# A long convolution and a feed-forward block on one core: a new early part, k and v in pieces, spectra of x in three groups, and a new written order

## The chip, the cores and the metric

The kernel runs on one core of a Trainium2 chip. The engines that matter here are TensorE (called PE in the profile, with its weight loads apart as PEld), VectorE (DVE), ScalarE (ACT), GpSimd (POOL) and SyncE (SP), which here only issues DMAs. The metric is device time in microseconds. The kernel before took 229.11 us, the median of three runs (227.98 to 230.42). The profile is of one further execution, which took 230.95 us.

## The reference, cut to what matters

The input `q` is [1, 2048, 640]; `k` and `v` have the same shape. All tensors are bf16.

```
def _A_ref(q, k, v, shift_k, ssm_k, ssm_D):
    # k_shift: four-tap causal filter of k along the sequence, a set of taps for each channel
    kv = k_shift * v
    # y: causal convolution of kv with ssm_k along the 2048 positions (by FFTs of length 4096)
    y = y + kv * ssm_D
    return q * y
def _B_ref(x, w1, b1, w2):          # 640 -> 1728 -> 640
    h = einsum("bsd,df->bsf", x, w1) + b1
    act = h * tanh(softplus(h))     # Mish
    return einsum("bsf,fd->bsd", act, w2)
x = q
h = x + _A_ref(_layernorm(x), k, v, shift_k, ssm_k, ssm_D)
out = h + _B_ref(_layernorm(h), w1, b1, w2)
```

## The kernel before, in words

The convolution is done as a Fourier transform by matmuls. The 2048 positions are split as 128 times 16, and the 640 channels into five chunks of 128, called `dc` 0 to 4. The filter `ssm_k` (called h) and the product kv (called x) go through the same two steps.

* `k1pe`: the filter's chunk (`kn`) is transposed, 16 transposes into one pair of PSUM banks; `k1ev` copies the two halves out to `kk`. Before that, `drow` turns the row `ssm_D` into a column with five one-column matmuls and `dadd` adds it to position 0 of the filter, so that the term `kv * ssm_D` costs nothing later.
* `s1pe` (line L280): step one, 16 matmuls for eight pairs of channels; four of these (`gi` 0 to 3) for each chunk. `s1ev` evicts a pair of banks (128x1024 in f32) to the buffer `B`.
* `s2pe` (L363): step two, one matmul for each of 128 frequencies and each group of chunks, against the matrix `G`, which `gb` builds from the table `R`. Chunks 0, 1 are one group of 64 columns, chunks 2, 3, 4 another of 96. `s2ev` evicts (128x1024 or 128x768) into `K` for the filter and into `X` for kv.
* `ktpe`/`ktev` (L314) transpose k; `shpe` (L333) does the four-tap filter with 32-row matmuls; `kv` (L341) multiplies by v on DVE and writes `kvb`, the input of step one for x.
* `d_sw`: DMAs within the chip's memory that write for each block of 16 channels a copy of the filter's spectrum with real and imaginary halves swapped (`KPS`). `pr` (L412, DVE) multiplies both copies by the spectrum of x; there are ten blocks of two halves.
* `i1pe` (L423, L424) and `i2pe` (L485) are the inverse transform, with evictions `i1ev` and `yev` (all evictions are line L185, on ACT or DVE).

Then come the rows. For each of 16 tiles T of 128 positions, `ln1` takes the statistics of x (L464), `lnx` normalises on ACT, `wb` and `h` form q*y and the residual, `ln2` takes statistics again, `dr` normalises, and the result is transposed: by PE for tiles 0 and 1 (`trpe`, `trev`), by DMA (`d_tr`, L553) for the others. The feed-forward block works in six units of 1, 1, 2, 4, 4, 4 tiles: `m1pe` (L573) and the activation `mi` (L580, ACT), then `m2pe` (L597), the last addition `res` (L616) and the store `d_o`.

PSUM has eight banks, used as four pairs for all evictions of 1024 columns (pair 0 is banks 0 and 1), or singly. A block of matmuls may start only when the pair it writes has been evicted.

The order of all this is not chosen at run time: a long string, `ORDER`, lists some 760 operations with their engine, their PSUM bank or pair, and for most DMAs an eviction behind which they are paced (`d_sw0_0:sp:@s1ev_h_4_0`). Each engine executes its operations strictly in that order; SP issues DMAs strictly in that order too, so a DMA that waits for its pace or its data holds up every later one. A dependence graph adds the semaphore waits.

```
for name, eng, slots, behind in _order():
    o = ops.pop(name)
    for x, s in zip(o.allocs, slots):
        x["slot"] = x["ring"][s]
    r = o.emit(eng)
    if behind:
        tc.add_manual_dep(r.ins, copies[behind].ins.name, info, reason="pace")
```

Of the kernel before, what the change touches and what calls it, by code (L numbers as in the profile page):

```python
# [15 lines left out]
P = 128  # L16
S = 2048
# [12 lines left out]
NGRP = len(GRP_DC)  # L30
KPE = 5
# [17 lines left out]
    "K": (O_K, 81920), "X0": (O_X, 16384), "X1": (O_KVB, 24576),  # L49
}  # L50
for _i, (_a, _b) in enumerate(GRP_DG):
    BUFS[f"B{_i}"] = (O_B + 256 * _a, 256 * (_b - _a))
# [117 lines left out]
def plan(v):  # L170
# [24 lines left out]
    def e_consts(e):  # L195
        v.nc.scalar.dma_start(v.consts[:], v.dram["consts"])
        v.nc.scalar.dma_start(v.buf("Drow", [P, D])[0:1], v.A_D.rearrange("(o d) -> o d", o=1))
    g.op("consts", "act", e_consts, w=["consts", "Drow"], kind="consts")
# [24 lines left out]
    if KPE:  # L223
        for h in range(2):
            dma(f"d_k{h}", 2048 * KC, lambda e, h=h: v.nc.sync.dma_start(
                v.buf("kna", [P, NT, KC])[:, 8 * h:8 * h + 8, :], v.A_k[0].rearrange("(p a) d -> p a d", a=NT)[:, 8 * h:8 * h + 8, 0:KC]), w=[("kna", h)])
    for h in range(2):
        dma(f"d_v{h}", 1.31e6, lambda e, h=h: v.nc.sync.dma_start(
            v.buf("v", [P, NT, D])[:, 8 * h:8 * h + 8, :], v.A_v[0].rearrange("(p a) d -> p a d", a=NT)[:, 8 * h:8 * h + 8, :]), w=[("v", h)])
# [6 lines left out]
    def e_pewarm(e):  # L236
        pw = bank(wrt)
        for i in range(8):
            v.nc.tensor.matmul(pw[:, 0:512], v.buf("warm", [P, 512])[:, 0:128], v.buf("warm", [P, 512]), start=True, stop=True)
# [6 lines left out]
    g.op("drow", "pe", e_drow, r=["Drow", "consts"], allocs=[drt], kind="drow")  # L246
# [9 lines left out]
    def e_pewarm2(e):  # L256
        for i in range(2):
# [3 lines left out]
    keep = g.op("pewarm2", "pe", e_pewarm2, r=["warm"], allocs=[wrt2], kind="pewarm2", after=[o for o in g.ops if o.name == "drow"])  # L261
# [4 lines left out]
    for i, (c0, c1) in enumerate(((0, 1), (1, 2), (2, 5))):  # L266
# [4 lines left out]
    def s1(st, dc, src, skey, bname, g0):  # L271
        for gi in range(4):
# [8 lines left out]
            g.op(f"s1pe_{st}_{dc}_{gi}", "pe", pe, r=["consts", (skey, gi // 2)], allocs=[rt], kind="s1pe")  # L281
# [6 lines left out]
    def k1(dc, grp):  # L288
        rt = alloc(D2)
        kk = f"kk{dc % 4}"  # L290

        def pe(e):
            pk = bank(rt, BF16).rearrange("p (t d) -> p t d", t=NT)
            for t2 in list(range(1, NT)) + [0]:
                v.nc.tensor.transpose(pk[:, t2, :], v.buf("kn", [P, NDC, S])[:, dc, t2:S:NT], v.ident)  # L295
        g.op(f"k1pe{dc}", "pe", pe, r=[("kn", dc), "consts"], allocs=[rt], kind="k1pe", after=[keep])
        for h in range(2):
            g.op(f"k1ev{dc}_{h}", EV, lambda e, h=h: ev(
                e, v.buf(kk, [P, 64, NT, 2])[:, 32 * h:32 * h + 32], bank(rt, BF16).rearrange("p (t d m) -> p d t m", t=NT, m=2)[:, 32 * h:32 * h + 32]),
                w=[(kk, h)], uses=[rt], kind="evb", arg=1024)  # L300
        s1("h", dc, lambda: v.buf(kk, [P, 64, NT, 2]), kk, f"B{grp}", GRP_DG[grp][0])
# [6 lines left out]
    for h in range(2):  # L308
        for dc in range(KPE):
# [5 lines left out]
            g.op(f"ktpe{dc}_{h}", "pe", pe, r=[("kna", h), "consts"], allocs=[rt], kind="ktpe")  # L315
# [36 lines left out]
    def s2(st, grp, dst, keys):  # L352

        d0, d1 = GRP_DG[grp]
        nd = d1 - d0
        nf, pitch, cost = SHAPE[nd]
        for ci in range(P // nf):
# [3 lines left out]
            def pe(e, rt=rt, f0=f0):  # L361
                for fl in range(nf):
                    v.nc.tensor.matmul(bank(rt)[:, fl * pitch:fl * pitch + nd], v.buf("G", [P, P, P])[:, f0 + fl, :], v.buf(f"B{grp}", [P, P, nd])[:, f0 + fl, :],  # L363
                                       start=True, stop=True)
            o = g.op(f"s2pe_{st}_{grp}_{ci}", "pe", pe, r=gall(f0, nf) + [f"B{grp}"], allocs=[rt], kind="s2pe", arg=nf * cost)
# [5 lines left out]
    def blocks(grp):  # L371
# [443 lines left out]
```

## Time and profile before

| what | value |
|---|---|
| median of three runs | 229.11 us (227.98 to 230.42) |
| the profiled execution | 230.95 us, its span 229.2 us |
| PE busy | 215.5 us (94%) |
| DVE busy | 149.0 us (65%) |
| ACT busy | 139.4 us (61%) |
| first eviction on ACT starts | 10.16 us |
| first matmul of the feed-forward block starts | 104.41 us |
| last matmul block ends | 225.8 us |

"Span" is from the first to the last instruction; the execution's own time is 1.75 us longer. Times in the trace count from the span's start. "Busy" of PE counts matmuls from their start to their modelled end, and as they are pipelined, a busy PE is not a PE at its peak. A timeline row gives start, length, engine, line, operation, shape and count, and in brackets the idle time ahead of it and who ended it. The granted clock is 1.00 in nearly all slices of the page, but the rate of the matmuls themselves tells more, as the prediction shows.

### The profile page before, as it was taken

The page shows a single profiled execution, that of the slowest core. Times are in us where ns is not written, and L with a number is a line of the kernel's source. Part 1 is how long each engine was busy: PE and PEld are TensorE (multiplying, and loading weights), DVE is VectorE, ACT ScalarE, POOL GpSimd, SP SyncE. Part 2 cuts the span into 40 slices and gives each one's busy share as a digit, 9 for nine tenths or more (in the row PEclk, how much of TensorE's full clock was granted, in tenths as well). Part 3 has the DMA queues.
Part 4 walks back from the last instruction along what each step waited for, and adds up shares of the span by engine and source line. Part 5 has one row for each costly group of instructions (what it writes and reads, how often), then busy time and mean ns, then how long its engine had stood idle before and what let it go on. Part 6 is the DMA issues. An engine that isn't in the chain of part 4 may idle for free.

```text
span 229.2 us, 6927 instructions
## 1 busy us (share of the span) xinstructions
PE 215.5 (94%) x3016; PEld 162.4 (71%) x3021; DVE 149.0 (65%) x274; ACT 139.4 (61%) x200; POOL 28.1 (12%) x60
## 2 busy tenths in 40 slices
PE   6899998979888999999999999999999999999994
PEld 2798888868787899998978764447557444577773
DVE  0469999999999999999999999965001200004131
ACT  2159998847999999999939367781350466100000
POOL 2120000000010000221233443522000000000000
PEclk9999999999999999999999999999999999999999
DMA  6999604845665777788230423424000100002021
GB/s 204 402 370 374 247 3 97 182 100 139 157 152 138 209 202 219 227 228 257 83 86 4 104 39 87 87 59 60 30 0 29 57 3 0 0 0 85 33 80 35
DMA packets 19872, 27.87 MB, mean 122 GB/s; under 512 B 10881, under 2 KB 14978, under 8 KB 19330
## 3 DMA queue, kind: packets, MB, share of 16 engines
q1 hardware_dynamic: 19536, 27.32, 41.0%
q8 instruction: 23, 0.38, 0.7%
q10 hardware_dynamic: 146, 0.11, 0.5%
q0 software_dynamic: 160, 0.01, 0.2%
q14 instruction: 7, 0.06, 0.1%
HBM read 17.27 MB, written 2.62 MB: 87 GB/s over the span
## 4 chain that ended last, share of the span: by engine, by line
PE 65%; ACT 14%; DVE 12%; DMA 4%; issue 3%; ACTq 0%; DVEq 0%
PE banks L597 26%; PE banks L573 23%; ACT arena L185 14%; PE banks L280 4%; DVE arena L412 4%; PE banks L363 3%; DVE arena L185 3%; PE banks L295 2%; DMA arena<-arena 2%; PE banks L333 2%; DMA arena<-in_A_ssm_D_dram 2%; DVE st L464 2%; DVE arena L341 2%; PE banks L576 1%; PE banks L485 1%
## 5 line engine op out<-in xcount | busy, mean ns | idle before, releaser
L185 ACT CAST arena<-banks 128x1024 bf16<-128x1024 f32 (+3 forms) x93 | 79.9, 985 | 16.5 <-PE banks L280 11.7
L597 PE MATMUL banks<-arena 128*128 128x320 bf16 (+2 forms) x448 | 61.7, 299 | 0.0
L580 ACT ACTIVATE arena<-banks,b1s 128x512 bf16<-128x512 f32 (+2 forms) x84 | 41.5, 535 | 29.7 <-PE banks L573 29.1
L573 PE MATMUL banks<-arena 128*128 128x512 bf16 (+2 forms) x395 | 58.2, 305 | 0.6 <-DVE nmr L473 0.3
L597 PEld LDWEIGHTS <-arena 128*128 128x128 bf16 x448 | 43.2, 98 | 18.1
L573 PEld LDWEIGHTS <-arena 128*128 128x128 bf16 x400 | 33.1, 98 | 23.7 <-issue 0.6
L616 DVE TENSOR_TENSOR arena<-banks,arena 128x640 bf16<-128x640 f32 x15 | 12.2, 816 | 56.4 <-PE banks L597 52.6
L185 DVE CAST arena<-banks 128x1024 bf16<-128x1024 f32 (+1 forms) x27 | 30.4, 1158 | 2.0 <-PE banks L280 1.3
L280 PE MATMUL banks<-consts,arena 128*64 128x128 bf16 x640 | 23.3, 230 | 2.6 <-ACT arena L185 1.1
L363 PE MATMUL banks<-arena 128*128 128x64 bf16 (+1 forms) x512 | 22.5, 199 | 2.7 <-ACT arena L185 2.4
L280 PEld LDWEIGHTS <-arena 128*64 128x64 bf16 x640 | 20.3, 116 | 4.7 <-issue 2.7
L363 PEld LDWEIGHTS <-arena 128*128 128x128 bf16 x512 | 19.9, 98 | 4.7 <-issue 3.6
L412 DVE TENSOR_TENSOR arena<-arena 128x2048 bf16<-128x2048 bf16 x20 | 22.9, 1216 | 0.2 <-DMA arena<-arena 0.2
L535 ACT ACTIVATE arena<-arena,nmr,r1v 128x640 bf16<-128x640 bf16 x16 | 14.3, 930 | 8.7 <-DVE nmr L473 7.5
L423 PE MATMUL banks<-a,arena 128*128 128x128 bf16 x160 | 18.8, 219 | 0.7 <-ACT arena L185 0.6
L424 PE MATMUL banks<-a,arena 128*128 128x128 bf16 x160 | 18.7, 219 | 0.0
L424 PEld LDWEIGHTS <-arena 128*128 128x128 bf16 x160 | 15.6, 98 | 0.9 <-issue 0.8
L423 PEld LDWEIGHTS <-arena 128*128 128x128 bf16 x160 | 15.6, 98 | 0.6 <-DVE arena L412 0.3
L185 DVE COPY arena<-banks 128x1024 bf16<-128x1024 bf16 (+1 forms) x17 | 10.7, 658 | 5.3 <-PE banks L295 4.5
L464 DVE BATCH_NORM_STATS2 st<-arena 128x6 f32<-128x320 bf16 x32 | 13.8, 474 | 0.0
L341 DVE TENSOR_TENSOR arena<-banks,arena 128x512 bf16<-128x512 f32 x20 | 12.3, 681 | 0.7 <-PE banks L333 0.3
L523 DVE BATCH_NORM_STATS2 st<-arena 128x6 f32<-128x320 bf16 x28 | 12.3, 480 | 0.2
(60 smaller groups left out, 139.6 us busy)
## 6 DMA issues: line engine op xcount, KB each, us to landing
arena<-arena SPq DMA_DIRECT2D x20, 256.0 KB, 3.0
arena<-in_A_ssm_k_dram SPq DMA_DIRECT2D x5, 512.0 KB, 6.4
arena<-in_A_k_dram SPq DMA_DIRECT2D x2, 1280.0 KB, 13.1
arena<-in_A_v_dram SPq DMA_DIRECT2D x2, 1280.0 KB, 19.6
arena<-in_A_q_dram SPq DMA_DIRECT2D x8, 320.0 KB, 3.2
out_dram<-arena SPq DMA_DIRECT2D x15, 160.0 KB, 1.8
arena<-in_B_w_dram SPq DMA_DIRECT2D x5, 432.0 KB, 4.4
arena<-in_B_w_dram SPq DMA_DIRECT2D x3, 480.0 KB, 5.1
```

What stands on the lines that cost most here:

```text
L185: v.copy = v.nc.scalar.copy(o, i) if e == "act" else v.nc.vector.tensor_copy(o, i)
L280: v.nc.tensor.matmul(pz[64 * ri:64 * ri + 64, gl, :], lhs, v.fcfs[:, ri, :], start=True, stop=True)
L341: v.nc.vector.tensor_tensor(v.buf(f"kvb{dc}", [P, 64, NT, 2])[:, q * 16:(q + 1) * 16], bank(rts[h])[:, i * 512:(i + 1) * 512].rearrange("p ...
L363: v.nc.tensor.matmul(bank(rt)[:, fl * pitch:fl * pitch + nd], v.buf("G", [P, P, P])[:, f0 + fl, :], v.buf(f"B{grp}", [P, P, nd])[:, f0 + f ...
L412: v.nc.vector.tensor_tensor(kk, xx.unsqueeze(1).to_broadcast([P, 2, 16, 64]), kk, ALU.mult)
L423: v.nc.tensor.matmul(pz[:, gl, :], v.buf(f"KP{b}", [P, 16, P])[:, 8 * h + gl, :], v.a12[:, 0, :], start=True, stop=False)
L424: v.nc.tensor.matmul(pz[:, gl, :], v.buf(f"KPS{b}", [P, 16, P])[:, 8 * h + gl, :], v.a12[:, 1, :], start=False, stop=True)
L464: v.nc.vector.bn_stats(v.st1[:, T % 4, q, :], x(T)[:, q * 320:(q + 1) * 320])
L535: g.op(f"lnx{T}", "act", lambda e: v.nc.scalar.activation(lnx(), x(T), ACT.Identity, scale=v.r1v[:, T:T + 1], bias=v.nmr1[:, T:T + 1]), r= ...
L573: v.nc.tensor.matmul(ph[:, 0:w], w1[:, dc, fc * P:(fc + 1) * P], lt[:, dc, T0 * P:T0 * P + w], start=(dc == 0), stop=(dc == NDC - 1))
L580: g.op(f"mi{u}_{fc}", "act", lambda e, fc=fc, rt=rt, ww=ww: v.nc.scalar.activation(ub()[:, fc, 0:ww], bank(rt)[:, 0:ww], ACT.Mish, bias=v. ...
L597: v.nc.tensor.matmul(bank(rt)[:, q * 512:q * 512 + b - a], lhs, w2()[:, wc, a:b], start=(fc == 0), stop=(fc == NFC - 1))
```

## The change

1. **The first chunk of the filter.** It is transposed in two blocks of eight (`k1pe0_0`, `k1pe0_1`) into single banks, each evicted by itself. Each copy covers half of the 16 values of the inner position for all channels, so all four `s1pe_h_0` blocks now need both copies. `ssm_D` is no longer added to this chunk ahead of the transposes; `dk0` adds the row to the evicted copy, in one partition, 128 elements. The other four chunks keep `drow` and `dadd`, and `drow` stands behind the first transposes.
2. **The warm-up.** Matmuls on a zeroed buffer run at the start: 8 and then 2 before (the 2 behind `drow`), 7 and 3 now, all ten in one go ahead of the first transposes.
3. **The identity apart.** The table `consts` came in one DMA; now the identity (128 columns) comes first in a DMA of its own, then `ssm_D`, then the rest.
4. **k and v** come in four DMAs each of 640 KB instead of two of 1280 KB, and those of k, v and `R` are no longer issued at once but paced behind evictions.
5. **The spectra of x** are made in three groups of chunks (0, 1 / 2, 3 / 4) of 64, 64 and 32 columns instead of two of 64 and 96. The filter keeps two groups. So `s2pe_x` has 384 matmuls instead of 256, and 20 evictions of 1024 columns instead of 8 of 1024 and 16 of 768.
6. **A new order** of everything, with the engine of many evictions chosen afresh. Up to the feed-forward block, two copies of `k1ev` and four more evictions of `s1ev` go from DVE to ACT, three copies of `ktev` from ACT to DVE, `trev0` (the first tile's transpose) to ACT, and two `yev2` evictions and three of the four `ln1` that stood there go behind it or change their place. `shpe4` and all of chunk 4 of x come late; one inverse block, `i2pe2_3`, now stands among the first unit's `m1pe` blocks; `m1pe` of the 4-tile unit of tiles 4 to 7 now follows one `m2pe` instead of two.

```
+X_DC = [[0, 1], [2, 3], [4]]
+X_DG = [(32 * c[0], 32 * c[-1] + 32) for c in X_DC]
...
-        v.nc.scalar.dma_start(v.consts[:], v.dram["consts"])
         v.nc.scalar.dma_start(v.buf("Drow", [P, D])[0:1], v.A_D.rearrange("(o d) -> o d", o=1))
+        v.nc.scalar.dma_start(v.consts[:, 128:424], v.dram["consts"][:, 128:424])
+    g.op("ident", "act", lambda e: v.nc.scalar.dma_start(v.consts[:, 0:128], v.dram["consts"][:, 0:128]), w=["ident"], kind="ident")
...
-        for h in range(2):
-            dma(f"d_k{h}", 2048 * KC, lambda e, h=h: v.nc.sync.dma_start(
-                v.buf("kna", [P, NT, KC])[:, 8 * h:8 * h + 8, :], ...
+        for h in range(4):
+            dma(f"d_k{h}", 1024 * KC, lambda e, h=h: v.nc.sync.dma_start(
+                v.buf("kna", [P, NT, KC])[:, 4 * h:4 * h + 4, :], ...
...
-        for i in range(8):
+        for i in range(7):
             v.nc.tensor.matmul(pw[:, 0:512], v.buf("warm", [P, 512])[:, 0:128], v.buf("warm", [P, 512]), start=True, stop=True)
...
-        for i in range(2):
+        for i in range(3):
...
-    keep = g.op("pewarm2", "pe", e_pewarm2, ..., after=[o for o in g.ops if o.name == "drow"])
+    keep = g.op("pewarm2", "pe", e_pewarm2, ..., after=[o for o in g.ops if o.name == "pewarm"])
...
-    for i, (c0, c1) in enumerate(((0, 1), (1, 2), (2, 5))):
+    for i, (c0, c1) in enumerate(((1, 2), (2, 5))):
...
+        if dc == 0:
+            for h in range(2):
+                rt = alloc(D1)
+                def pe(e, rt=rt, h=h):
+                    pk = bank(rt, BF16).rearrange("p (t d) -> p t d", t=8)
+                    for t2 in range(8 * h, 8 * h + 8):
+                        v.nc.tensor.transpose(pk[:, t2 - 8 * h, :], v.buf("kn", [P, NDC, S])[:, dc, t2:S:NT], v.ident)
+                g.op(f"k1pe{dc}_{h}", "pe", pe, r=[("kn", dc), "ident"], allocs=[rt], kind="k1pe", arg=8, after=[keep])
+                g.op(f"k1ev{dc}_{h}", EV, lambda e, h=h, rt=rt: ev(
+                    e, v.buf(kk, [P, 64, NT, 2])[:, :, 8 * h:8 * h + 8], bank(rt, BF16).rearrange("p (t d m) -> p d t m", t=8, m=2)),
+                    w=[(kk, ("t", h))], uses=[rt], kind="evb", arg=1024)
+            g.op("dk0", "dve", lambda e: v.nc.vector.tensor_tensor(
+                v.buf(kk, [P, 64, NT, 2])[0:1, :, 0, :], v.buf(kk, [P, 64, NT, 2])[0:1, :, 0, :],
+                v.buf("Drow", [P, D])[0:1, 0:128].rearrange("p (d m) -> p d m", m=2), ALU.add), r=["Drow"], w=[(kk, ("t", 0))], kind="tiny")
...
-        d0, d1 = GRP_DG[grp]
+        d0, d1 = (GRP_DG if st == "h" else X_DG)[grp]
...
-    for grp in range(NGRP):
-        d0, d1 = GRP_DG[grp]
+    for grp in range(len(X_DC)):
+        d0, d1 = X_DG[grp]
```

The new order begins as follows, against the old one's first lines:

```
-    d_kn0:sp consts:act small:pool warmset:dve d_kn2:sp pewarm:pe:0 tab:act d_kn4:sp d_kn1:sp d_kn3:sp d_k0:sp d_R0:sp d_k1:sp d_R1:sp drow:pe:0
-    d_v1:sp pewarm2:pe:1 dadd0:dve k1pe0:pe:1 d_v0:sp k1ev0_0:dve k1ev0_1:dve s1pe_h_0_0:pe:3 d_a12:sp s1pe_h_0_1:pe:0 s1ev_h_0_0:act diag:dve
+    ident:act consts:act tab:act small:pool d_kn0:sp warmset:dve d_kn2:sp pewarm:pe:0 d_kn1:sp d_kn4:sp d_kn3:sp pewarm2:pe:0 k1pe0_0:pe:1
+    k1pe0_1:pe:2 k1ev0_0:dve drow:pe:3 k1ev0_1:dve dk0:dve s1pe_h_0_3:pe:1 s1pe_h_0_0:pe:0 s1ev_h_0_3:act dadd0:dve diag:dve s1pe_h_0_2:pe:2
+    d_R0:sp:@k1ev0_1 s1ev_h_0_0:act s1ev_h_0_2:dve k1pe1:pe:1 s1pe_h_0_1:pe:0 k1ev1_0:dve s1ev_h_0_1:act dadd1:dve k1ev1_1:dve s1pe_h_1_1:pe:2
```

## The prediction

> **What bounds it now.** I read the busy time by stretches first: up to the first eviction's stage, the middle of the convolution, its later half, the feed-forward block.
>
> ```profile
> 9.00:57.00 48.00, 43.61 (x1274) 40.19 (x1276) 42.87 (x61) 37.30 (x43) 2.52 (x4) 1.00 0.64 201
> 57.00:104.40 47.40, 44.53 (x836) 41.11 (x831) 46.25 (x64) 47.36 (x58) 3.79 (x7) 1.00 0.72 191
> 104.40:225.80 121.40, 120.80 (x885) 77.92 (x887) 58.45 (x147) 53.24 (x100) 19.66 (x42) 1.00 0.21 54
> ```
>
> The columns are PE, PEld, DVE, ACT, POOL, granted clock, DMA share, GB/s. From 104.4 on PE has no gap: that part can't get shorter, and begins when it may. From 57 to 104.4 ACT is busy 47.36 of 47.40 us, DVE 46.25, PE 44.53: three full engines, ACT the fullest. Before 57 ACT loses time, so I went to its timeline.
>
> ```profile
> 10.16 1.01 ACT L185 CAST arena<-banks 128x1024 bf16<-128x1024 f32 x1 [6.89 <-PE banks L280]
> 11.87 1.93 ACT L185 CAST arena<-banks 128x1024 bf16<-128x1024 f32 x2 [0.69 <-PE banks L280]
> 15.72 1.01 ACT L185 CAST arena<-banks 128x1024 bf16<-128x1024 f32 x1 [1.93 <-PE banks L280]
> 17.44 7.61 ACT L185 CAST arena<-banks 128x1024 bf16<-128x1024 f32 x8 [0.70 <-PE banks L280]
> ...
> 37.87 6.60 ACT L185 CAST arena<-banks 128x768 bf16<-128x768 f32 x9 [0.78 <-PE banks L363]
> 45.23 1.71 ACT L185 CAST arena<-banks 128x768 bf16<-128x768 f32 x2 [0.77 <-PE banks L363]
> 49.97 2.63 ACT L185 CAST arena<-banks 128x768 bf16<-128x768 f32 x3 [3.02 <-PE banks L363]
> 53.19 2.84 ACT L185 CAST arena<-banks 128x1024 bf16<-128x1024 f32 x3 [0.59 <-PE banks L280]
> 56.92 3.76 ACT L185 CAST arena<-banks 128x1024 bf16<-128x1024 f32 x4 [0.88 <-PE banks L280]
> ```
>
> So the start of the feed-forward block, 104.4, is ACT's first eviction (10.16) plus its work plus its idle time: 3.3 us of idle up to 17.4 and 6.0 from there to 57, all waiting for PE. Each of these is a term below. Why PE is late at first is in its timeline:
>
> ```profile
> 5.32 0.28 PE L245 MATMUL banks<-consts,arena 1*128 1x1 bf16 x5 [0.54 <-DMA arena<-in_A_ssm_D_dram]
> 5.53 1.03 PE L258 MATMUL banks<-arena 128*128 128x512 bf16 x2
> 6.36 1.91 PE L295 MATMUL banks<-consts,arena 128*128 128x128 bf16 x16
> 9.06 3.62 PE L280 MATMUL banks<-consts,arena 128*64 128x128 bf16 x64 [0.78 <-DVE arena L185]
> ...
> 16.76 1.08 PE L280 MATMUL banks<-consts,arena 128*64 128x128 bf16 x32
> ```
>
> 64 matmuls of step one take 3.62 us at 9.06, so a block of 16 takes 0.90; at 16.76, 32 take 1.08, a block 0.55. The starts in the trace change pace at 13.38: transposes come every 107 ns up to there and every 62 ns behind it. PE thus runs at half rate for 13.4 us, though it began to work at 1.18: it paused at 4.8 (waiting for `ssm_D`) and at 8.3 (for the copies).
>
> **The change, term by term, on ACT's path.**
>
> *First eviction.* Ten warm-up matmuls at the cold pitch of 0.427 us run from 1.18 to 5.45. The filter's first chunk is there (a 512 KB row issued at 0.72 takes 4.4 us), and the identity, issued first, is smaller than the whole table that landed in 3.9 us. 16 transposes at 107 ns end by 7.2, at 62 ns from 6.5 on by 6.9. The first copy (0.69 us, L185) runs beside the second eight; the second ends at 7.9, `dk0` (near the 0.15 us of the old `dadd`, 0.08 without overlap) at 8.0. Step one then starts at 8.0 instead of 9.06, and its first eviction follows after 0.72 us if PE is warm, 1.10 if cold (10.16 less 9.06): 8.75 or 9.1. **Minus 1.4**, at least minus 0.9. The new layout of the two copies isn't in the trace; between the 0.69 us of the old one and the 1.22 of an f32 eviction I take 0.69, the same 1024 bf16.
>
> *PE warm.* PE now works without a pause from 1.2 to about 7. The Trainium skill ("TensorE: Matmul & The Clock Gate", the HAM clock gate) says that the clock is doubled after one busy window of 3.4 us of a free-running counter, so not at a fixed time from the start; the flip here fits, since the stretch of 3.4 us that ended at 13.38 is the first without a pause. By the trace alone: 3.6 us of work (1.18 to 4.77) was not enough, 4.3 us (9.06 to 13.38) was, and the new stretch has 5.7. If it is warm from 7, step one's four blocks shrink by 1.3 us (3.62 to 4 x 0.57) and the next 32 transposes by 0.4 (2.44 in the chain, to 2 x 1.0): 1.7 of the 3.3 idle. **Minus 1.6**, between 0 and minus 3.
>
> *Work.* 8 evictions of 1024 and 16 of 768 become 20 of 1024. In the trace ACT starts one every 0.91 us or every 0.69 us when it has no wait: 18.3 us against 18.2, nothing. Adding up the two written lists with such pitches (DVE: 0.60 for a bf16 copy, 1.14 for an f32 one, 1.2 for a `kv`, 1.135 for a `pr`, 1.04 for a `ln1`), ACT has 0.5 us less ahead of the block (82.5 against 83.0). DVE has 84.4 us up to `dr0` instead of 87.0, and no longer does `ln1_2`, `dr1` and `trev0` (1.8) before the block. As ACT is the fuller, **minus 0.5**; if the work could be spread evenly, minus 2.
>
> *Middle idle (6.0 us).* The longest, 3.02, is a block of step two that stands in PE's order behind `shpe3`, which waits for banks that `kv2` on DVE still reads. All five `shpe` blocks and their ten `kv` (0.68 us each half, 1.2 with its pair) stay, and each can stop PE again; they now stand apart. I walked the new lists with these durations and find pauses of 0.4 to 1.1 at `shpe2`, `shpe3`, `shpe0` and one of about 0.7 while v is waited for. **Minus 1.0**, between plus 1.5 and minus 3. Cover: the pieces of k and v must land in time (a rival below).
>
> *Three groups.* 128 of the 256 matmuls with 96 columns (42 ns from start to start) become 64-column ones (29 ns), minus 1.7 us of PE, and 128 of 32 columns come on top. Their pitch is nowhere in the trace: at least the 14 ns of L333's 32-row ones, at most the 98 ns of an uncovered weight load. The nearest row is the 64-column form's 29: plus 3.7. So PE gets 2.0 us more in a stretch where it has 2.9 spare. In return the products of eight blocks don't wait for chunk 4. **Plus 0.8**, between 0 and 8.
>
> *Feed-forward.* `i2pe2_3` (8 matmuls, 0.45 us) now stands in it. Tiles 2 and 3 leave no slack: after `dr0` DVE's list has 14.9 us up to the second of `dr2`, `dr3` (13.2 before), then two transposing DMAs:
>
> ```profile
> 115.31 2.63 SPq L553 DMA_TRANSPOSE arena<-arena x2
> 120.36 7.26 PE L573 MATMUL banks<-arena 128*128 128x256 bf16 x65
> ```
>
> They landed at 119.3, 1.1 us ahead of the matmuls; now I get 0.3 to 0.5 behind them. The unit after it is needed 3.8 us sooner, with DVE's list up to it 3.6 us shorter. **Plus 0.9**, between 0.45 and 3. The tail is unchanged in shape.
>
> *Sum:* -1.4 - 1.6 - 0.5 - 1.0 + 0.8 + 0.9 = -2.8. The block starts near 100.7; the execution takes 230.95 - 2.8 = 228.15, which is 1.84 above the median of the runs for the same kernel, so **226.3** in those terms.
>
> **Rivals** (times in terms of the median).
>
> *The warm-up misses.* The rows bound the stretch of work that PE needs between 3.6 and 4.3 us, but one execution can't tell that it isn't also a matter of when the stretch begins. If PE stays cold past 7, as it did until 13.4, the 1.6 and 0.4 of the first eviction come back: 228.3. By the skill's rule just named, this happens whenever no whole window of the free-running counter falls between 1.2 and 7: as an estimate it must begin within 2.4 of its 3.4 us, a miss in 3 of 10 executions, fewer for a median. **0.13**
>
> *The pieces come late.* k and v are paced now; `v2` is issued behind `ktev1_1`, 4.7 us of DVE's list ahead of `kv1_1`, which needs all of v, and 480 KB rows took 5.1 us. If three waits (for k's two halves and for v) cost 0.8 us each: 228.7. **0.12** Against it, the five 512 KB pieces of the filter ran at 370 to 402 GB/s in the page's slices. The Trainium skill speaks for it: "DMA: Bandwidth & Descriptors", Bandwidth, asks for 1 MiB in a DMA; by its table, as an estimate, 640 KB pieces run at 300 GB/s instead of 341, and k and v end 2.1 us later. The slices show no such loss.
>
> *No gain in the middle.* The stalls only move: the middle gives +0.5 instead of -1.0, the three groups +1.5, and tiles 2 to 7 wait 1 us more: 229.5. This is also the case in which the order doesn't do what it says. **0.13**
>
> *Slower.* The 32-column matmuls are held by their 128-column weight loads. At 98 ns, 128 of them take 12.5 us, PE gets 10.8 us more between 57 and the block, 2.9 are spare: 7.9 on the path in place of 0.8, so 233.4. It decides from 64 ns each: then 6.5 more, 3.6 on the path, no gain left. Against it: 29 ns in the 64-column form, with loads of the same size. At a middle 75 ns: 230.5. **0.12**
>
> *Forecast*, 226.3, its own range 224.4 to 227.9: **0.50**.
>
> The range that should hold 8 in 10 reaches from 224.2 over the first three rivals to 230.6. One per cent, 2.3 us, is about what a measurement of this kernel can tell from none. Faster by over 1% (under 226.8): most of the forecast and a little of the first rival, 0.46. Within: 0.35. Slower: 0.19.
>
> **What would show it.** Right: L280's first block at 8.0 with 0.55 to 0.6 us each; ACT's first eviction at 8.8; ACT's idle up to 57 near 6.5 us; L363's 32-column form near 29 ns; the first `m1pe` near 100.7 and PE gapless behind it but for a pause before the 256-column form. Wrong: 0.9 us blocks after 8, waits of `ktpe` or `kv` for DMA, ACT idle between 57 and 100, or PE waits for `d_tr`.

## The result, and the profile after

The changed kernel takes **229.95 us** (median of 20 executions, 228.98 to 231.57). The kernel before, run beside it, takes 228.67 us (20 executions, 227.93 to 230.42). The ratio is **1.0055, 95% interval 1.0034 to 1.0077**: slower by 0.55%, less than the 1% that the forecast called a difference. The forecast was 226.3. The time lies inside the range (224.2 to 230.6), but the gain of 2.8 us didn't come, and a loss of 1.3 came instead.

The two profiled executions alone would have told the opposite. The one of before took 230.95 us, more than any of the 20 executions timed beside the changed kernel. The one of after took 229.84.

First the busy time by stretches of the kernel after, with the columns that the prediction explained (PE, PEld, DVE, ACT, POOL, granted clock, DMA share, GB/s):

```profile
9.00:57.00 48.00, 42.24 (x1245) 38.89 (x1241) 41.53 (x56) 40.20 (x45) 3.46 (x4) 1.00 0.72 209
57.00:104.40 47.40, 44.99 (x996) 42.25 (x991) 45.44 (x66) 46.56 (x54) 4.84 (x8) 1.00 0.68 190
104.40:225.80 121.40, 120.39 (x880) 77.26 (x876) 58.29 (x148) 52.78 (x97) 19.34 (x42) 1.00 0.20 52
```

Up to 57, ACT does 2.9 us more than before (40.20 against 37.30), so there is less idle time before 57. It went at the start, not in the middle: from 17.44, where the prediction divided ACT's idle time, to 57 ACT is busy no more than before. The columns are the same; first before, then after:

```profile
17.44:57.00 39.56, 35.22 (x1130) 32.20 (x1126) 37.11 (x51) 33.35 (x39) 0.14 (x1) 1.00 0.56 160
```

```profile
17.44:57.00 39.56, 34.30 (x1066) 31.45 (x1066) 34.90 (x47) 32.88 (x38) 0.00 (x0) 1.00 0.73 211
```

The stretch from 57 on is nearly as full as it was (ACT 46.56 us against 47.36). ACT's timeline, the same view as before:

```profile
9.22 1.93 ACT L189 CAST arena<-banks 128x1024 bf16<-128x1024 f32 x2 [5.58 <-PE banks L285]
12.05 4.68 ACT L189 CAST arena<-banks 128x1024 bf16<-128x1024 f32 x5 [0.90 <-PE banks L285]
...
27.74 1.01 ACT L189 COPY arena<-banks 128x1024 bf16<-128x1024 bf16 x1 [1.36 <-PE banks L336]
29.55 4.69 ACT L189 CAST arena<-banks 128x1024 bf16<-128x1024 f32 x5 [0.80 <-PE banks L385]
```

The gap of 3.02 us of before is gone; the longest is now 1.36. The first eviction starts at 9.22, not at the forecast 8.75. Why is in PE's timeline of the kernel after:

```profile
5.45 1.38 PE L303 MATMUL banks<-consts,arena 128*128 128x128 bf16 x16
6.77 0.27 PE L250 MATMUL banks<-consts,arena 1*128 1x1 bf16 x5
8.55 1.53 PE L285 MATMUL banks<-consts,arena 128*64 128x128 bf16 x48 [1.51 <-DMA consts<-tab_consts]
10.29 1.16 PE L317 MATMUL banks<-consts,arena 128*128 128x128 bf16 x16 [0.21 <-ACT arena L189]
```

The full rate is there: 48 matmuls of step one take 1.53 us. But they begin at 8.55, behind a wait of 1.51 us for the rest of the table `consts`.

The feed-forward block has no pause worth naming in either kernel. In after its first matmul starts at 103.24 and its last ends at 224.97, 121.72 us later, against 121.36 before. Tiles 2 and 3 came in time: the form with 256 columns follows PE's work without a wait.

```profile
111.94 7.77 PE L619 MATMUL banks<-arena 128*128 128x320 bf16 x56
119.55 2.67 PE L595 MATMUL banks<-arena 128*128 128x256 bf16 x23
```

### The profile page after: what moved, and what is told of

Read it like the earlier page. It is cut to its first block, busy times and chain, and to the rows that moved or that the text cites. A ratio compares the mean times of both kernels' runs of the same rounds, so it can differ in the third digit from the quotient of the medians.

```text
span 228.1 us, 7204 instructions
## 1 busy us (share of the span) xinstructions
PE 213.9 (94%) x3149; PEld 161.9 (71%) x3149; DVE 147.5 (65%) x274; ACT 141.0 (62%) x196; POOL 29.3 (13%) x60
## 4 chain that ended last, share of the span: by engine, by line
PE 64%; DVE 13%; DMA 9%; ACT 9%; issue 3%; POOL 1%; ACTq 0%; DVEq 0%; POOLq 0%
PE banks L619 26%; PE banks L595 23%; ACT arena L189 8%; PE banks L385 4%; PE banks L285 4%; DMA arena<-in_A_k_dram 3%; DMA arena<-arena 3%; DMA consts<-tab_consts 3%; DVE arena L189 3%; DVE arena L434 3%; DVE st L486 2%; DVE arena L363 2%; PE banks L317 2%; PE banks L355 2%; PE banks L598 1%
## 5 line engine op out<-in xcount | busy, mean ns | idle before, releaser
L189 ACT CAST arena<-banks 128x1024 bf16<-128x1024 f32 (+1 forms) x89 | 80.5, 1008 | 11.9 <-PE banks L285 8.2
L602 ACT ACTIVATE arena<-banks,b1s 128x512 bf16<-128x512 f32 (+2 forms) x84 | 42.2, 534 | 38.6 <-PE banks L595 37.8
L595 PE MATMUL banks<-arena 128*128 128x512 bf16 (+2 forms) x400 | 58.8, 306 | 0.2 <-DVE arena L189 0.2
L619 PEld LDWEIGHTS <-arena 128*128 128x128 bf16 x448 | 43.2, 98 | 18.1
L595 PEld LDWEIGHTS <-arena 128*128 128x128 bf16 x400 | 33.2, 98 | 23.7 <-issue 0.8
L189 DVE CAST arena<-banks 128x1024 bf16<-128x1024 f32 (+3 forms) x27 | 28.8, 1109 | 1.2 <-PE banks L285 0.6
L285 PE MATMUL banks<-consts,arena 128*64 128x128 bf16 x640 | 21.8, 220 | 3.5 <-DMA consts<-tab_consts 1.5
L385 PE MATMUL banks<-arena 128*128 128x64 bf16 (+2 forms) x640 | 23.9, 192 | 1.2 <-ACT arena L189 0.5
L385 PEld LDWEIGHTS <-arena 128*128 128x128 bf16 x640 | 21.6, 97 | 2.7 <-issue 1.5
L285 PEld LDWEIGHTS <-arena 128*64 128x64 bf16 x640 | 19.1, 110 | 5.2 <-issue 2.5
L445 PEld LDWEIGHTS <-arena 128*128 128x128 bf16 x160 | 15.5, 98 | 1.7 <-DVE arena L434 1.5
L446 PEld LDWEIGHTS <-arena 128*128 128x128 bf16 x160 | 15.6, 98 | 0.0
```

Source lines behind the costliest of these rows:

```text
L189: v.copy = v.nc.scalar.copy(o, i) if e == "act" else v.nc.vector.tensor_copy(o, i)
L285: v.nc.tensor.matmul(pz[64 * ri:64 * ri + 64, gl, :], lhs, v.fcfs[:, ri, :], start=True, stop=True)
L445: v.nc.tensor.matmul(pz[:, gl, :], v.buf(f"KP{b}", [P, 16, P])[:, 8 * h + gl, :], v.a12[:, 0, :], start=True, stop=False)
L446: v.nc.tensor.matmul(pz[:, gl, :], v.buf(f"KPS{b}", [P, 16, P])[:, 8 * h + gl, :], v.a12[:, 1, :], start=False, stop=True)
L595: v.nc.tensor.matmul(ph[:, 0:w], w1[:, dc, fc * P:(fc + 1) * P], lt[:, dc, T0 * P:T0 * P + w], start=(dc == 0), stop=(dc == NDC - 1))
L602: g.op(f"mi{u}_{fc}", "act", lambda e, fc=fc, rt=rt, ww=ww: v.nc.scalar.activation(ub()[:, fc, 0:ww], bank(rt)[:, 0:ww], ACT.Mish, bias=v. ...
```

## The experiments

Each ratio is against the kernel before, run beside it on the same chip. The runs come from four chips, where the median of before was 228.68 to 228.97, so times of different chips are best compared by their ratios. Some kernels differ from each other by less than their intervals; where that is so, the text says it. Each execution also comes with its mean granted clock of TensorE, which one group below uses.

### What an early full rate is worth

The kernel before once more, one execution.

> The kernel before once more, for a second profile of it. The first one took 230.95 us, 2.3 above the median of twenty runs (228.67), and its matmuls went from half to full rate at 13.38 us. Theory A (the moment at which the matmuls reach full rate differs from execution to execution, and a late one is what made the first profile slow): near 228.5 us, with full rate clearly ahead of 13 us, and a first eviction on ACT before 10 us. Rival B (full rate always comes near 13 us here): again at 12.5 to 15 us, and 228 to 231 us.

It took 229.9 us (span 228.1), 1.05 us less than the first profiled execution of the same kernel, but not the 228.5 of theory A: it is still 0.9 over the median of before on that chip (228.97), so only its early part can stand for a usual execution. PE's timeline of this second execution of before:

```profile
5.24 0.60 PE L258 MATMUL banks<-arena 128*128 128x512 bf16 x2
5.68 1.15 PE L295 MATMUL banks<-consts,arena 128*128 128x128 bf16 x16
7.61 1.53 PE L280 MATMUL banks<-consts,arena 128*64 128x128 bf16 x48 [0.78 <-DVE arena L185]
```

16 transposes take 1.15 us, where the first profile showed 1.91; step one starts at 7.61 and not 9.06, at full rate; the first eviction starts at 8.29 and not 10.16. So the same kernel gets the full rate at about 5 us in one execution and at 13.4 in another. Which of them is the usual one, the next run tells: the warm-up of the change alone, in the kernel before.

```
-        for i in range(8):
+        for i in range(7):
...
-        for i in range(2):
+        for i in range(3):
...
-    ... d_R1:sp drow:pe:0
-    d_v1:sp pewarm2:pe:1 dadd0:dve ...
+    ... d_R1:sp pewarm2:pe:1
+    d_v1:sp drow:pe:0 dadd0:dve ...
```

> The kernel before with the changed kernel's warm-up alone: ten matmuls in one go ahead of drow, nothing else. Theory A (the full rate comes late in most executions of the kernel before): full rate near 6 us, step one's first four blocks in 2.3 instead of 3.6 us, 226.8 to 227.5 us against 228.67. Rival C (a typical execution of the kernel before is already at full rate early, only its first profile wasn't): 228.2 to 229.0 us, no difference.

228.77 us, ratio 0.9995 (0.9969 to 1.0021). Step one starts at 7.67 and the first eviction at 8.35: no better than what before reaches by itself in the execution just shown. Ten warm-ups without a pause buy nothing at the median. The opposite, before with hardly any warm-up (one matmul for eight, one for two):

```
-        for i in range(8):
+        for i in range(1):
...
-        for i in range(2):
+        for i in range(1):
```

> The kernel before with one warm-up matmul in each of the two places instead of eight and two, so that TensorE stands idle for most of the first 5 us. Leaves out only the warm-up work. Theory (the moment of the full rate differs between executions when the warm-up is as long as it is here, and a late one costs about 1 us: 230.95 in the first profile, with the full rate from 13.4, against 229.9 in the second, with it from 4.6): the full rate comes behind 9.5 us in every execution, the first eviction at 9.9 to 10.2, and the time is 0.8 to 1.2 us over the kernel before, 1.0035 to 1.005. Rival (a late full rate costs what the forecast gave it, 1.6 us and the 0.4 of the first eviction, 2.0 in all): 1.008 to 1.010. Second rival (the delay is taken up later, and the slow first profile was something else): 1.000 to 1.002.

230.54 us, ratio 1.0076 (1.0050 to 1.0101), 1.8 us over before. PE's timeline of this run has the half rate that the first profile of before had, 64 matmuls in 3.62 us:

```profile
5.87 1.91 PE L295 MATMUL banks<-consts,arena 128*128 128x128 bf16 x16
8.57 3.62 PE L280 MATMUL banks<-consts,arena 128*64 128x128 bf16 x64 [0.79 <-DVE arena L185]
```

So a late full rate costs 1.8 us, nearer to the forecast's 2.0 than to the 1.0 that I had read off two profiles. The price was right. It just isn't paid in most executions of before, or their median would be near that of this run instead of 1.8 us below; so it couldn't be saved. (When the rate comes is seen in profiles alone; for the other executions it is inferred from their times.)

### The divided table

Before, with only the table divided as in the change (the main lines; the transposes and `drow` also wait for `ident` alone now):

```
-        v.nc.scalar.dma_start(v.consts[:], v.dram["consts"])
         v.nc.scalar.dma_start(v.buf("Drow", [P, D])[0:1], v.A_D.rearrange("(o d) -> o d", o=1))
+        v.nc.scalar.dma_start(v.consts[:, 128:424], v.dram["consts"][:, 128:424])
+    g.op("ident", "act", lambda e: v.nc.scalar.dma_start(v.consts[:, 0:128], v.dram["consts"][:, 0:128]), w=["ident"], kind="ident")
```

> The kernel before with only the table divided as in the change: identity, then ssm_D, then the rest. Theory (the rest of the table, issued third, lands behind the filter's pieces at 8.5, and step one needs it): step one starts at 8.5 instead of 7.6, the first eviction at 9.2 instead of 8.3, and 0.4 to 0.9 us more, 1.002 to 1.004. Rival (the order behind it takes the delay up, as the filter's pieces are late as well): 0.999 to 1.001.

229.54 us, ratio **1.0036 (1.0015 to 1.0056)**, 0.8 us. PE's timeline of this run:

```profile
5.42 1.16 PE L296 MATMUL banks<-consts,arena 128*128 128x128 bf16 x16
8.50 3.58 PE L281 MATMUL banks<-consts,arena 128*64 128x128 bf16 x64 [1.92 <-DMA consts<-tab_consts]
```

Two things are in it. Step one starts at 8.50, 0.9 us later than in the second execution of before: the rest of the table (74 KB) is issued third on ACT's queue, while the filter's pieces are loading, and takes 6.7 us to land, where the whole table (106 KB), issued first, took 3.9. And the transposes ahead of the wait ran at full rate (16 in 1.16 us), but step one behind it runs at half rate (64 in 3.58): the pause lost the rate again. The windows of the same run have the granted clock (the third figure from the end):

```profile
6.00:9.00 3.00, 1.08 (x21) 1.05 (x20) 1.62 (x3) 0.00 (x0) 0.04 (x1) 0.91 1.03 369
9.00:12.00 3.00, 3.00 (x59) 2.88 (x55) 1.85 (x4) 1.70 (x2) 0.94 (x1) 0.52 1.06 439
12.00:15.00 3.00, 3.00 (x55) 2.84 (x53) 1.74 (x3) 1.42 (x3) 0.00 (x0) 1.00 1.02 324
```

Half the clock for 3.4 us of 228 is a mean of 0.993, and that number picks such executions out; in two of them, this run and the one with `R` early below, a profile shows the loss, in the others it is inferred from the clock. Of the kernels with the divided table and nothing in its wait, 17 of 68 timed executions have 0.993 or less (7 of the 20 of the changed kernel). With the table in one DMA they are 2 of 72, and of before 0 of 122. In the changed kernel those seven take 230.78 us (median), the other thirteen 229.56: one such loss costs 1.2 us.

The changed kernel with its table in one DMA, ahead of `ssm_D`, its loads paced as they were:

```
-        v.nc.scalar.dma_start(v.consts[:, 128:424], v.dram["consts"][:, 128:424])
-    g.op("ident", "act", lambda e: v.nc.scalar.dma_start(v.consts[:, 0:128], v.dram["consts"][:, 0:128]), w=["ident"], kind="ident")
+    g.op("ident", "act", lambda e: v.nc.scalar.dma_start(v.consts[:], v.dram["consts"]), w=["ident"], kind="ident")
```

> The changed kernel with the table consts in one DMA ahead of the row ssm_D, as before, instead of the identity first and the rest behind the row. The rest landed at 8.51 us and step one waited for it until 8.55. If that wait counts: step one starts near 7.9 us and the execution gains 0.5 to 0.7 us: 229.3. If the paced loads decide (theory P, since each is issued behind an eviction, they too come earlier by the same): 0.3 to 0.6 us. If the waits for R and k behind it take it up (rival): no difference, 229.9.

229.37 us, ratio 1.0005 (0.9974 to 1.0036): the table alone is worth about as much as the whole loss, though the intervals of the two kernels just touch. Step one starts at 7.61 and the first eviction at 8.29. That is the start that before reaches with its old first block (7.61, 8.29), so the two halves of the first block buy nothing here: in their place step one waits 0.8 us for `dk0`, where before waited 0.8 for the copies.

Two more runs fill the wait for the table with six matmuls on the zeroed buffer, so that the rate can't fall back while the wait stays; first in the changed kernel, then in before with the divided table.

```
+    g.op("pewarm3", "pe", e_pewarm3, r=["warm"], allocs=[wrt3], kind="pewarm3", after=[o for o in g.ops if o.name == "drow"])
...
-    ... k1ev0_0:dve drow:pe:3 k1ev0_1:dve ...
+    ... k1ev0_0:dve drow:pe:3 pewarm3:pe:0 k1ev0_1:dve ...
```

> The changed kernel with six more warm-up matmuls behind drow, in the 1.6 us in which TensorE waits for the rest of the table. Theory (in part of the executions the pause lets the rate fall back, which costs 1.1 us each time): no half-rate matmuls behind 8.5, the upper half of the times goes, median 0.3 to 0.6 us under the changed kernel, 1.002 to 1.004, and no time over 230.5. Rival (the rate falls back too seldom to matter; the wait and the paced loads are the cost): 1.0045 to 1.006.

> The kernel before with the table divided, and six more warm-up matmuls behind the first transposes, in the 1.9 us wait. Theory (as in the run before): 1.0015 to 1.003 instead of 1.0036, no half-rate matmuls behind 8.5. Rival: 1.003 to 1.005.

The first gave 229.73 us, 1.0046 (1.0026 to 1.0067), the second 229.31 us, 1.0018 (1.0000 to 1.0036). In neither did the mean clock of an execution go below 0.997 (0 of 24), so filling the wait does hold the rate. In before with the divided table 0.4 us of 0.8 came back, which is not clear of noise (the intervals overlap). In the changed kernel hardly any did, as the rival had it: its executions at a clock of 1.00 took 229.83 us (9 of them), no less than the 229.56 of the changed kernel's undisturbed ones. My expectation that no time would be over 230.5 failed (three were, up to 230.98). What the filling costs in the executions in which the first full rate comes late wasn't measured apart.

### The paced loads

The changed kernel with the eviction taken away behind which each early load was paced; the order of the loads stays.

```
-    d_R0:sp:@k1ev0_1 ... d_v3:sp:@k1ev1_1 ... d_k2:sp:@s1ev_h_1_0 ... d_R1:sp:@k1ev4_0 ... d_k3:sp:@s1ev_h_2_0
+    d_R0:sp ... d_v3:sp ... d_k2:sp ... d_R1:sp ... d_k3:sp
```

> The changed kernel with the loads of R, k, v and the table a12 issued at once, in the same order, instead of paced behind evictions. Theory P (the pacing leaves the DMA engines empty from 11.5 to 15 us, so that R's second half and k's last piece land 3 us late, and the lists carry these 3 us to the end): DVE's wait for R (3.05 us) and PE's wait for k (2.3 us) are gone, the feed-forward block starts 2 to 3 us earlier, 227.0 to 227.9 us, below the kernel before by 0.3 to 0.8%. Rival Q (the time is lost later, in the three saturated engines, and the early waits only take the place of others): 229.4 to 230.2 us.

229.14 us, ratio 1.0005 (0.9975 to 1.0035), between the two expectations and in neither. What pacing does shows in the windows around 12 us: of the kernel before, of the kernel after, and of this run.

```profile
11.50:15.00 3.50, 3.50 (x56) 3.31 (x50) 1.75 (x5) 1.93 (x2) 0.00 (x0) 1.00 1.00 332
```

```profile
11.50:15.00 3.50, 3.21 (x84) 2.89 (x84) 3.45 (x6) 2.95 (x4) 1.58 (x2) 1.00 0.36 68
```

```profile
11.50:15.00 3.50, 3.22 (x83) 2.94 (x81) 3.50 (x7) 3.43 (x4) 0.00 (x0) 1.00 1.01 336
```

The paced kernel leaves the DMA engines nearly empty for 3.5 us (68 GB/s instead of 332), because the filter's pieces have landed and the next load may not be issued yet. Those 3.5 us of loading are then missing: DVE and PE of the kernel after wait for loads.

```profile
DVE arena L256 <- DMA arena<-tab_R: 3.0, 1, 3.0
```

```profile
PE banks L336 <- DMA arena<-in_A_k_dram: 2.3, 1, 2.3
PE banks L285 <- DMA consts<-tab_consts: 1.5, 1, 1.5
```

Without pacing both of the long ones are gone. But other waits stand in their place: PE waits 1.5 us for evictions by DVE (0.2 in the paced kernel), DVE 2.2 for ACT (1.3), and ACT's idle time up to the block is 7.7 us against 8.4 and 7.7 in two profiles of the changed kernel. Which of the two waits was the dearer, the changed kernel with the second half of `R` behind the first tells:

```
-    d_R0:sp:@k1ev0_1 ... d_R1:sp:@k1ev4_0 ...
+    d_R0:sp:@k1ev0_1 d_R1:sp ...
```

> The changed kernel with the second half of R issued right behind the first, all else paced as it was. Theory (the 3.05 us in which DVE waits for R's second half is the dearer of the two waits, since the eviction list behind it is full): more than half of what the pacing costs goes, 0.6 to 0.9 us less than the changed kernel, 1.002 to 1.003. Rival (the wait of PE for a piece of k is what counts, or the loads behind are later by as much): the time of the changed kernel within 0.3 us, 1.004 to 1.007, with the wait for k 1.4 us longer or so.

229.13 us, ratio 1.0021 (0.9993 to 1.0050): the wait for `R` is gone, those for k are 0.9 us in all. The changed kernel itself, beside it on the same chip:

> The changed kernel once more, for comparison with the next three on the same chip. Theory (paced loads of k, v and R cost about 1.1 us and the divided table about 0.5, the rest of the change is worth about nothing): 1.004 to 1.008 of the kernel before, with DVE waiting 3 us for the second half of R and PE 2.3 us for a piece of k. Rival (the 0.55% of the first comparison is within what one session differs from the next): 1.000 to 1.003.

229.93 us, ratio **1.0050 (1.0025 to 1.0075)**, as in the first comparison, with waits of 2.5 us for `R` and 1.5 for k. So moving one load by 11 us is worth 0.6 us of the 1.1 by the medians, but the two intervals overlap. Part of what these two runs gained is chance: 4 of the 12 executions of the changed kernel had lost the rate, and 1 of these 12. Among executions at a clock of 1.00 the medians are 229.35 (changed), 229.07 (`R` early) and 229.05 (unpaced, on another chip), so pacing itself costs about 0.3 us by these medians and 0.5 by their ratios to before. That is no more than a hint: the executions of one kernel at full clock differ by more than 1 us.

Both doubtful parts undone, table in one DMA and no pacing:

> The changed kernel with both doubtful parts undone: consts comes in one DMA again, and k, v and R are issued at once. Theory (the two costs lie in different stretches and add up): 1.1 + 0.5 us less than the changed kernel, 228.3 where that is 229.95, so 0.997 to 0.999 of the kernel before. Rival (both delays end in the same later wait, so that undoing one hides the other): no better than the changed kernel without pacing alone, 1.0005. Second rival (step one starts earlier, but waits at the same place for the loads that are now issued at once): 1.000 to 1.003.

229.40 us, ratio 1.0026 (1.0010 to 1.0043). Undoing either part alone had given 1.0005, on another chip. The two gains don't add up; the second rival comes nearest. Step one starts at 7.93, and then PE waits three times for evictions by DVE, 2.2 us in all. Why the kernel with the table mended and the loads paced has a median of 228.69 among its executions at full clock (on another chip), and this one 229.40, stays open.

### ACT's work

In the last kernel PE and DVE wait for no load of k, v or `R` and no execution lost the rate, and still it is 0.7 us over before. The windows from the first eviction to the first matmul of the feed-forward block, of before and then of after:

```profile
10.16:104.41 94.25, 87.04 (x2086) 80.20 (x2083) 87.97 (x122) 84.67 (x100) 5.74 (x10) 1.00 0.67 193
```

```profile
9.22:103.24 94.02, 85.86 (x2204) 79.77 (x2199) 85.70 (x116) 85.59 (x96) 7.39 (x10) 1.00 0.70 200
```

ACT is busy 84.67 us before and 85.59 after (84.4 to 84.9 and 85.6 to 85.9 in all other profiles with the same lists of ACT): 1.0 us more, where the forecast had 0.5 less. DVE has 2.3 less. The two largest groups of ACT in these windows, in before and in after:

```profile
L185 ACT CAST arena<-banks 128x1024 bf16<-128x1024 f32 x63 | 60.4, 1067 | 11.8 <-PE banks L280 11.7
L185 ACT CAST arena<-banks 128x768 bf16<-128x768 f32 x26 | 19.2, 840 | 4.6 <-PE banks L363 4.6
```

```profile
L189 ACT CAST arena<-banks 128x1024 bf16<-128x1024 f32 x77 | 72.0, 1044 | 9.7 <-PE banks L285 8.2 <-PE banks L385 1.2
L189 ACT CAST arena<-banks 128x768 bf16<-128x768 f32 x10 | 7.7, 802 | 2.2 <-PE banks L385 1.9
```

ACT has 16 evictions of 768 fewer (15 of the 16 that the change removes had been on it, and one of the filter's went to DVE) and 14 of 1024 more. The busy times of two groups count what overlaps between them twice. Counted from each start to the next, the 14 add 12.5 us, the 16 take off 10.9, and ACT's other work is 0.7 less: 0.9 in all. To see whether ACT's work is what remains, the last kernel with two copies of the filter's third chunk back on DVE, where before has them:

```
-    ... k1ev2_0:act k1ev3_0:dve ... k1ev2_1:act k1ev4_0:dve ...
+    ... k1ev2_0:dve k1ev3_0:dve ... k1ev2_1:dve k1ev4_0:dve ...
```

> The changed kernel with its table in one DMA and its loads not paced (the kernel that gave 1.0026), and the two copies of k1ev2 back on DVE, where the kernel before has them. ACT gets 1.8 us less to do ahead of the feed-forward block, DVE 1.2 more. Theory (what is left over the kernel before is ACT's work, 86.6 us against 85.2 up to the block): ACT busy 84.8 up to the block, and 0.4 to 0.9 us less time, 0.998 to 1.001. Rival (the copies lie in a stretch in which both engines wait for PE, so that the place is free and idle time takes it): 1.002 to 1.004.

**228.25 us, ratio 0.9984 (0.9964 to 1.0003)**: 0.42% or 1.0 us less than without the move, by two ratios from two chips whose intervals do not overlap, for 1.8 us less of ACT's work. Its window:

```profile
8.97:102.88 93.91, 85.75 (x2206) 79.80 (x2201) 86.68 (x118) 83.84 (x94) 6.41 (x10) 1.00 0.68 198
```

Two more copies of k moved to DVE as well:

```
-    ... ktev4_1:act ... ktev3_0:act ...
+    ... ktev4_1:dve ... ktev3_0:dve ...
```

> The kernel that gave 0.9984 (changed, table in one DMA, loads not paced, k1ev2 on DVE) with ktev4_1 and ktev3_0 on DVE too. ACT gets 1.8 us less again, DVE 1.2 more. Theory (ACT's work is still the longer list): 0.3 to 0.8 us less, 0.995 to 0.997, faster than both kernels. Rival (with 83.8 us ACT has become the emptier one, and DVE's list, 86.7, is what counts now): 0.998 to 1.002.

228.71 us, ratio 0.9985 (0.9964 to 1.0006), no further gain. ACT is down to 82.1 us and waits 12.3, DVE up to 88.1: ACT is no longer the longer list. And the first tile's transposed copy back on DVE, ahead of `ln1_2`, first alone, then with the two copies:

```
-    hB1:dve ln1_2:dve trpe0:pe:1 i2pe1_1:pe:1 yev2_1:act ln1_3:dve trev0:act
+    hB1:dve trpe0:pe:1 trev0:dve ln1_2:dve i2pe1_1:pe:1 yev2_1:act ln1_3:dve
```

> The kernel that gave 1.0026 (changed, table in one DMA, loads not paced), with trev0 on DVE ahead of ln1_2, where the trace has it free, instead of on ACT. Theory (PE, not ACT, sets the start of the feed-forward block in the last 7 us ahead of it: 52 plus 16 matmuls of the inverse without a gap but the 0.37 at the transposes): the block starts 0 to 0.2 us sooner, 1.001 to 1.003. Rival (the block waits for trev0 on ACT, which ended 0.05 us ahead of its first matmul): 0.5 to 0.8 us sooner, 0.999 to 1.000.

> Both moves of the last two runs in one kernel. Theory (ACT's work is what is too much): 0.5 to 1.0 us less than 1.0026, 0.998 to 1.000, and possibly the fastest of all. Rival (neither is on the path): 1.002 to 1.003.

229.74 us (1.0048, 1.0030 to 1.0067) and 229.76 us (1.0049, 1.0029 to 1.0069). The second is clearly dearer than the kernel without `trev0` on DVE (0.9984, same chip); the first is dearer than its own (1.0026), with overlapping intervals. All readings missed. PE now waits inside the feed-forward block, for tile 1:

```profile
PE banks L570 <- DVE arena L562: 1.3, 2, 0.9
```

The block got 1.2 us longer (122.90 from its first matmul to the last, against 121.72): `dr1`, which the second tile's transposes need, stands behind `trev0`, four `ln1` and the second tile's own statistics in DVE's list, and the 0.4 us put ahead of it, with PE there sooner, turn into a wait of 0.9. In these lists `trev0` had room on ACT and none on DVE. The pair also limits the result before: the same move of the two copies that was worth 0.42% with `trev0` on ACT is worth nothing here (1.0048 and 1.0049).

## Why the prediction was wrong, step by step

**The sum was made against an unlucky execution, and its luck was taken off twice.** The step that failed most is "the execution takes 230.95 - 2.8 = 228.15, which is 1.84 above the median of the runs for the same kernel, so 226.3". The two early terms, -1.4 and -1.6, removed what made that execution slow: the first eviction at 10.16 and the half rate up to 13.4. The median execution of before has neither, as far as the runs tell (8.29 and about 5 in the second profile; warm-up alone 0.9995; hardly any warm-up 1.0076). Taking 3.0 off for them and then 1.84 more for the distance to the median counts one lateness twice. Against the median, the other four terms are what was left: -0.5 - 1.0 + 0.8 + 0.9 = +0.2. That the price of the late rate was sized well (1.8 measured) didn't help.

The sum fails even against the slow execution it was read from. From the first profile of before to that of after, the last matmul block ends 0.8 us sooner (225.8 against 225.0), not 2.8. The first eviction gave 0.9 of the 1.4, the stretch from there to the feed-forward block 0.2 where the terms had 2.3 (-1.6 - 0.5 - 1.0 + 0.8), and the block itself became 0.4 longer. Term by term, the stretch lost at "Work" and "Middle idle".

**First eviction, -1.4.** "Step one then starts at 8.0" is the sentence that failed, for a reason of its own. I checked the identity, which the transposes need, and forgot that step one reads the rest of the same table, which the change moved to third place. The table landed at 8.5. Against the usual execution of before the first eviction is 0.9 us later (9.22 against 8.3), and the divided table alone costs 0.8 (1.0036).

**PE warm, -1.6.** PE did work without a pause from 1.2 to about 7 and got its full rate at 5.8 to 6.0, as forecast; the rival that it would miss fell in both profiles. But the bounds for the work that PE needs, 3.6 to 4.3 us, don't hold. In other profiles with the same warm-up, begun at 1.21, the full rate was there at 4.02 (loads not paced), or not yet at 7.05 (the kernel of 0.9984), after 2.8 us of work and after more than 5.8. Nor was the stretch ahead of 13.38 the first without a pause: that from 1.18 to 4.77 has 3.6 us. And the rate took little of ACT's idle time that it was to take. Ahead of 17.44 ACT idles 3.3 us in the first profile of before, still 3.4 in the second and 2.6 with the new warm-up, both with the full rate early; in the changed kernel it is 0.9 in both profiles. So the new early part removed most of it; which piece of it did, no run isolates. Not foreseen: in 7 of 20 executions the rate was lost again in the pause behind it, at 1.2 us each, 0.4 us on average.

**Work, -0.5.** Measured +1.0, the worst-sized term of those that were really there. I set 82.5 us of ACT's list against 83.0, but the 83.0 ran over the last two evictions (1.0 us), which in the trace of before end at and behind the block's first matmul (the last one of after also ends behind it); and the remaining 768-column evictions, which I put at 0.69 each, took 0.77 on average, because they seldom follow each other without a gap now. What such work costs is shown for one kernel only: 1.0 us for two copies moved with `trev0` on ACT, nothing with `trev0` on DVE.

**Middle idle, -1.0.** It didn't come. ACT's idle time from the first eviction to the block is 8.4 and 7.7 us in the two profiles of the changed kernel, against 9.6, 10.4 and 9.2 in three of before and of before with the new warm-up: 1.7 less. But all of that lies ahead of 17.44. From 17.44 to 57, where the term was read, ACT idles 6.7 and 6.0 us against 6.2, 6.3 and 6.4, and from 57 to the block 0.8 and 0.9 against 0.0, 0.7 and 0.2. The pause of 3.02 us is gone and shorter ones stand in its place. Nor did its "Cover" hold, that the pieces of k and v land in time; yet without pacing the middle idles 5.9 us, so most of those waits took the place of others.

**Three groups, +0.8.** The 32-column matmuls start every 25 ns, where I took 29 from the 64-column form, so PE gets 1.5 us more and not 2.0. The Trainium skill ("TensorE: Matmul & The Clock Gate", "Wait — 56ns, not 53.3ns?") gives just this 25 ns as the least from start to start in its 32-column case. The trace agrees. What the groups alone cost in time wasn't tried; ACT's 0.8 us of idle time behind 57 may be theirs. The rival on the slow side needed 64 ns and fell.

**Feed-forward, +0.9.** Measured +0.36 (121.36 to 121.72), about what the inverse block that was put there takes (0.45). Tiles 2 and 3 were not late.

**The pieces come late** happened through the pacing, which the rival named, but the longest wait was one it didn't count: DVE's 3.0 us for the second half of `R`. The small size of the pieces had no part in it. Unpaced, the same pieces of 640 KB moved 336 to 402 GB/s from 11.5 to 18 us, beside 332 to 420 for the larger ones of before, so the loss that the Trainium skill's rule of 1 MiB a DMA ("DMA: Bandwidth & Descriptors", Bandwidth) would give isn't in this trace. The loss was in the gap in the issuing.

In sum, for medians: +0.9 for the first eviction, -0.5 from there to the block (93.7 us on average of two profiles, against 94.2 of five of before and of before with another warm-up or table), +0.36 in the block and +0.4 for the lost rate make 1.2; 1.28 was measured. The stretch to the block differs by up to 1.5 us between executions of one kernel (95.07 and 93.61 for before without and with the new warm-up), so single tenths of this sum are not shown. Best shown is the divided table, which costs before 0.8 us and, undone, brings the changed kernel to 1.0005. The time came nearest to the rival without a gain in the middle (229.5), and the middle did bring none. But that is in part luck: the rival's wait of tiles 2 to 7 didn't come, and it had neither the wait for the table, nor the lost rate, nor ACT's extra work.

## What to carry to other kernels

Before a term is read from the start of a profile, ask whether the median execution has it: an execution slower than all timed ones is slow for a reason, and that reason must not be saved a second time. When a table is divided so that one part comes sooner, list every reader of the other part. And where loads are paced behind evictions, read the GB/s of the stretch in which the first loads have landed: here it fell from 332 to 68.

## What the runs showed of the hardware

* The same kernel gets the full matmul rate at about 5 us or at 13.4. A late one costs 1.8 us here. With ten warm-up matmuls in one go from 1.21 it was there at 4.02 in one profile, at 5.98 in another and not yet at 7.05 in a third.
* With a pause of 1.5 to 1.9 us behind the first transposes (five profiles) the rate was lost again in 17 of 68 executions, for about 3.4 us, by the mean clock; with the pause filled, in 0 of 24. With pauses of 0.8 us it was 2 of 72 in the changed kernel with its table in one DMA and the kernels made from it, and 0 of 122 in before. The Trainium skill ("TensorE: Matmul & The Clock Gate", the HAM clock gate) speaks of an idle window of about 3.4 us, of a free-running counter. The duration of the loss agrees with it (in the profile of the kernel with `R` early the half rate lasted from 8.4 to 11.9 us). The pauses were only half as long as that window, and here the measurement decides: they sufficed in one execution of four.
* A mean granted clock of 0.993 marks such an execution without a trace: half the rate for 3.4 us of 228. A late first rate doesn't show in it (0.998 in the profile with the rate at 13.4).
* 74 KB issued third on ACT's queue, while SP's queue loaded the filter's 2.5 MB, took 6.7 us to land, and 106 KB issued first took 3.9.
